# Chunk 0 of a windowed-attention kernel: first loads in 4 KB rows, attention ahead of the weight conversions, and half of the weight subtractions moved from GpSimd to VectorE

## The chip, the cores and the metric

The kernel runs on one core of one Trainium2 chip. The metric is the device time of one execution in microseconds (us). In the text PE is TensorE, DVE is VectorE, ACT is ScalarE, POOL is GpSimd, and SP is SyncE, which issues the DMAs.

## What is computed

The reference is attention followed by a feed-forward block, all in float32. For each of 4 batches and 8 heads, 768 queries of 64 elements attend to the keys less than 16 positions away and to 24 summaries of the keys (the elementwise maximum over blocks of 32; the values' summary is the mean):

```python
k_sum = k.reshape(B, H, nb, block, D).max(axis=3)
v_sum = v.reshape(B, H, nb, block, D).mean(axis=3)
scores_l = scale * np.matmul(q, k.transpose(0, 1, 3, 2))          # kept where |i - j| < 16
scores_s = scale * np.einsum('bhsd,bhnd->bhsn', q, k_sum) + np.log(block)
a = softmax(np.concatenate([scores_l_masked, scores_s], axis=-1))
x = np.matmul(a, np.concatenate([v, v_sum], axis=2))              # 3072 tokens x 512
r = np.maximum(x @ w_in, 0.0)                                     # w_in 512 x 2048
out = (s * (r * r) + b) @ w_out                                   # w_out 2048 x 512
```

## The kernel before

**Tiling.** The 3072 tokens are 12 chunks `c` of 256 tokens, three for each batch. The 8 heads are 4 pairs `p`; a pair of heads of one chunk is a unit. The 2048 hidden features are 16 blocks `f` of 128.

**Attention of a unit** goes through the engines in these steps; the letters are those of the string `FIRST_ORDER`, and a digit behind a letter is the unit's `p`. K (`k_max`, L158): DVE takes the maxima of the keys. S (`scores`, L241): PE. M (`masked`, L264): DVE adds the mask and takes the maximum. E (`exps`, L281): ACT. N (`normalize`, L289): DVE divides by the sums. F (`fill_v`, L233): the 24 mean values are copied into the tile of values. T (`transposes`, L297): PE. C (`turned`, L303): ACT copies the transposed probabilities from PSUM. V (`values`, L307): PE. X (`attended`, L320): ACT copies the result, a block of x; from chunk 1 on it is split into a high part `xh` and a rest `xl`, which DVE subtracts. For chunk 0 the means of the values come from twelve matmuls over plain rows of v (R, `mean_of_rows`, L196) with one ACT copy behind them.

**Feed-forward.** For a chunk and an `f`, `hidden` (L335) multiplies x by a block of w_in, `activate` (L349) makes g = s r^2 + b, and `project` (L367) adds g times a block of w_out into two PSUM banks; `evict` (L384) stores them after f = 15. Chunk 0 uses whole float32 weights `w_f` and float32 x. From chunk 1 on there are three matmuls of a faster kind in place of one: with the rounded weight `wh` and its rest `wl`, and x and g split alike.

**Weights** arrive as 64-bit numbers, one block of w_in ("in") and one of w_out ("out") for each f, 512 KB each. `scale_weights` (L113; A in the string) is two ACT operations, `convert_weights` (L121; D for both halves of an f) is three DVE operations for each half (L132, L134, L136). `split_weights` (L138) later makes `wh` on ACT (L145) and `wl` by a subtraction (L147): on DVE for "in", on POOL for "out".

**Order.** The program is a plan of numbered steps; step i holds `hidden(c, f)` for i = 16 c + f, the `activate` of the same, and `project` of the one two steps back. The engines run their own instructions in the plan's order. Within a step the kinds follow each other as L393 says: loads, weight work (scaling, conversion, splitting), attention, hidden, PE's attention, activate, project, evict. Conversion of f stands at step f - 2, scaling at f - 3, splitting at 13 + f. The attention of chunk 1 is spread over steps 0 to 15, that of chunk c > 1 begins at step 16 (c - 1) - 2. Ahead of step 0 all loads of chunk 0 and the first twelve weights are issued on SP (L401 to L408), then the work in the string `FIRST_ORDER` (L397) is run.

**Buffers.** The pool `slots` has 16 buffers of 4 KB a partition: first the rows of v and the raw weights, later the pairs of rounded weights. `wring` holds the converted weights and the rests; the rest of an "out" block goes into the buffer of the "in" block of the same f.

Of the kernel before, what the change touches and what calls it, by code (L numbers as in the profile page):

```python
# [44 lines left out]
def windowed_attention_then_relu2_ffn(ctx, tc, qk, vwin, kt, vt, vrow, wp, s, b, out):  # L45
# [92 lines left out]
    def split_weights(key):  # L138
# [8 lines left out]
        (nc.vector if key[0] == "in" else nc.gpsimd).tensor_tensor(  # L147
# [10 lines left out]
    def k_max(bi, p):  # L158
        ksum[bi, p] = p2.tile([P, NB], F32, name="ksum", bufs=8)
        raw = kraw[bi, p]  # L160
        nc.vector.tensor_reduce(
            ksum[bi, p], raw.rearrange("p (n t) -> p n t", t=BLOCK), axis=AX.X, op=ALU.max
        )
# [25 lines left out]
    def load_rows():  # L189

        for j in range(3):
            t = slots.tile([P, 2, DM], F32, name="vn", tag="slot")
            nc.sync.dma_start(t, vrow[:, 2 * j : 2 * j + 2, :])
            vn.append(t)

    def mean_of_rows():  # L196
        pm = ps_po.tile([P, DM], F32, name="pm", tag="po")
        for j in range(6):
            nc.tensor.matmul(
                pm[:KR], mean4[:, 20 - 4 * j : 20 - 4 * j + KR], vn[j // 2][:, j % 2],  # L200
                start=(j == 0), stop=(j == 5),
            )
# [1 line left out]
        nc.scalar.copy(vsum[0][WIN:KR].rearrange("p h d -> p (h d)"), pm[WIN:KR])
# [327 lines left out]
```

## Time and profile before

| | |
|---|---|
| three runs | 668.0 us median (667.82 to 669.35) |
| the profiled execution's own time | 667.75 us |
| its span, first to last instruction | 666.1 us |
| busy: PE, DVE, ACT, POOL | 637.8, 327.3, 331.7, 173.2 us |
| read from memory, written | 55.90 MB, 6.29 MB |
| 16 subtractions `wl_out` on POOL (L147) | 23.2 us, 1451 ns each |

The profile is of one execution. A row of a timeline gives the start, the duration, engine, line, operation, the tile written and those read, the shape, and in brackets how long the engine was idle before it and for what it waited. A row of the chain of waits gives the start, the time that this piece adds to the chain, and the piece. A group of instructions has its busy time and the mean of one, then the idle time before its instructions and who ended it. In a timeline two instructions of one engine can overlap by a pipeline's length, so that an engine's pace is read from starts, or from the chain.

### The profile page before, as it was taken

Reading aid. Unit: us, or ns where it says so; the run is one execution under the profiler, and the core shown is the slowest. Engines: PE = TensorE matmul, PEld = TensorE weight load, DVE = VectorE, ACT = ScalarE, POOL = GpSimd, SP = SyncE. Lnnn points to the kernel's source line nnn. Section 1 sums busy time; section 2 is a strip of 40 time slices with the busy share of each in tenths; the row PEclk is TensorE's granted clock in tenths of the full one; section 3 lists DMA queues with packets and bytes.
Section 4 is the critical chain, followed back from the end, with each engine's and each line's share of the span. In section 5 each row is a group of like instructions: output and inputs, shape, how many; then the busy total and the mean of one; then the engine's idle time right before and its main releaser. Section 6 shows DMA issues by size and latency. Waiting matters only on the chain.

```text
span 666.1 us, 13961 instructions
## 1 busy us (share of the span) xinstructions
PE 637.8 (96%) x5164; PEld 555.1 (83%) x5164; DVE 327.3 (49%) x1086; ACT 331.7 (50%) x972; POOL 173.2 (26%) x342
## 2 busy tenths in 40 slices
PE   4698989989999999999999999999999999999997
PEld 2465657878999999999989999999999999999996
DVE  2799995467443343346543343345643343443221
ACT  2598967564444444444444444444543543543322
POOL 3000034553322312313313313313313313312221
PEclk9798999989999999999999999999999999999999
DMA  7999602304510320503520320503520320100000
GB/s 235 357 378 372 190 1 80 102 1 124 172 59 2 106 66 1 180 1 104 181 70 2 102 70 1 180 1 100 185 71 1 101 71 1 57 2 2 31 1 32
DMA packets 26100, 63.25 MB, mean 95 GB/s; under 512 B 3952, under 2 KB 4464, under 8 KB 26032
## 3 DMA queue, kind: packets, MB, share of 16 engines
q1 hardware_dynamic: 25968, 62.35, 28.6%
q8 instruction: 41, 0.67, 0.4%
q14 instruction: 27, 0.22, 0.1%
q0 software_dynamic: 64, 0.00, 0.0%
HBM read 55.90 MB, written 6.29 MB: 93 GB/s over the span
## 4 chain that ended last, share of the span: by engine, by line
PE 82%; DVE 9%; ACT 3%; DMA 2%; POOL 1%; issue 1%; SPq 1%; POOLq 0%; ACTq 0%
PE po L379 37%; PE ph L345 36%; PE pav L315 4%; PE pt L301 3%; PE ps L258 3%; DMA kraw<-in_kt_dram 2%; DVE wf_out L136 1%; DVE wf_out L134 1%; DVE wf_in L134 1%; DVE wf_in L136 1%; DVE pr L295 1%; DVE pr L272 1%; ACT pr L285 1%; POOL wl_out L147 1%; DVE wl_in L147 1%
## 5 line engine op out<-in xcount | busy, mean ns | idle before, releaser
L352 ACT ACTIVATE r<-ph 128x256 f32<-128x256 f32 x192 | 73.3, 382 | 293.2 <-PE ph L345 255.8
L362 DVE CAST gh<-g 128x256 fp32r<-128x256 f32 x176 | 52.2, 297 | 302.5 <-POOL g L360 283.9
L360 POOL TENSOR_SCALAR g<-r,s_col,b_col 128x256 f32<-128x256 f32 x176 | 99.7, 567 | 374.4 <-ACT r L353 318.0
L379 PE MATMUL po<-wh,gl 128*128 128x512 f32 x352 | 143.6, 408 | 0.0
L379 PE MATMUL po<-wh,gh 128*128 128x512 f32 x352 | 139.1, 395 | 0.0
L379 PE MATMUL po<-wl_out,gh 128*128 128x512 f32 x352 | 138.4, 393 | 0.0
L345 PEld LDWEIGHTS ph<-xh,wl_in 128*128 128x128 f32 x704 | 108.1, 189 | 16.2 <-ACT r L353 0.7
L345 PE MATMUL ph<-xh,wl_in 128*128 128x256 f32 x704 | 113.5, 284 | 0.0
L345 PE MATMUL ph<-xl,wh 128*128 128x256 f32 x704 | 109.3, 277 | 0.0
L345 PE MATMUL ph<-xh,wh 128*128 128x256 f32 x704 | 108.8, 277 | 0.0
L345 PEld LDWEIGHTS ph<-xl,wh 128*128 128x128 f32 x704 | 95.3, 189 | 0.0
L345 PEld LDWEIGHTS ph<-xh,wh 128*128 128x128 f32 x704 | 92.9, 188 | 0.0
L353 ACT ACTIVATE r<-r 128x256 f32<-128x256 f32 x192 | 80.2, 418 | 6.1
L285 ACT ACTIVATE pr<-pr,mn 128x120 f32<-128x120 f32 x192 | 73.2, 383 | 14.0 <-DVE mn L272 14.0
L364 DVE TENSOR_TENSOR gl<-g,gh 128x256 fp32r<-128x256 f32 x176 | 76.5, 435 | 6.0
L379 PEld LDWEIGHTS po<-wh,gh 128*128 128x128 f32 x352 | 66.4, 189 | 14.0
L379 PEld LDWEIGHTS po<-wh,gl 128*128 128x128 f32 x352 | 66.4, 189 | 10.8 <-DVE gh L362 2.7
L379 PEld LDWEIGHTS po<-wl_out,gh 128*128 128x128 f32 x352 | 66.6, 189 | 7.9
L147 POOL TENSOR_TENSOR wl_out<-wf_out,wh 128x512 fp32r<-128x512 f32 x16 | 23.2, 1451 | 108.9 <-ACT wh L145 83.8
L301 PE MATMUL pt<-ident,pr 128*120 128x128 f32 x192 | 30.5, 283 | 9.2 <-DVE pr L295 9.1
L295 DVE TENSOR_TENSOR pr<-pr,rs 128x480 f32<-128x480 f32 x48 | 35.5, 741 | 1.7
L285 ACT ACTIVATION_READ_ACCUMULATOR pr<-pr,mn 128x1 f32 x192 | 36.0, 188 | 0.0
(67 smaller groups left out, 621.9 us busy)
## 6 DMA issues: line engine op xcount, KB each, us to landing
wraw<-in_wp_dram SPq DMA_DIRECT2D x32, 512.0 KB, 10.2
qk<-in_qk_dram SPq DMA_DIRECT2D x44, 368.0 KB, 4.8
vw<-in_vwin_dram SPq DMA_DIRECT2D x48, 192.0 KB, 4.1
kraw<-in_kt_dram SPq DMA_DIRECT2D x16, 384.0 KB, 3.4
out_dram<-o SPq DMA_DIRECT2D x24, 256.0 KB, 2.0
vraw<-in_vt_dram SPq DMA_DIRECT2D x12, 252.0 KB, 4.4
vraw<-in_vt_dram SPq DMA_DIRECT2D x6, 264.0 KB, 6.7
vn<-in_vrow_dram SPq DMA_DIRECT2D x3, 512.0 KB, 10.6
```

What stands on the lines that cost most here:

```text
L147: (nc.vector if key[0] == "in" else nc.gpsimd).tensor_tensor(w_l[key], whole, w_h[key].bitcast(F32), ALU.subtract)
L285: nc.scalar.activation(pr, pr, AF.Exp, bias=mn_of[c, p][:, n : n + 1], scale=-1.0, accum_out=sm_of[c, p][:, n : n + 1])
L295: nc.vector.tensor_tensor(pr, pr, rs.unsqueeze(2).to_broadcast([P, 4, KR]), ALU.mult)
L301: nc.tensor.transpose(pt_of[c, p][:KR, n * P : (n + 1) * P], pr[:, n, :], ident)
L315: nc.tensor.matmul(o[64 * e : 64 * e + 64, i * SUB : (i + 1) * SUB], vw[:, e, i, :], pT[:, e * T + i * SUB : e * T + (i + 1) * SUB], start ...
L345: nc.tensor.matmul(ph, w[:, kc * P : (kc + 1) * P], x[:, kc], start=(n == 0), stop=(n == len(terms) - 1))
L352: nc.scalar.activation(r, ph, AF.Relu)
L353: nc.scalar.activation(r, r, AF.Square)
L360: nc.gpsimd.tensor_scalar(g, r, s_col, b_col, ALU.mult, ALU.add)
L362: nc.vector.tensor_copy(gh, g)
L364: nc.vector.tensor_tensor(gl, g, gh.bitcast(F32), ALU.subtract)
L379: nc.tensor.matmul(po[t], a[:, t * P : (t + 1) * P], w, start=(f == 0 and n == 0), stop=(f == NF - 1 and n == len(terms) - 1),)
```

## The change

It has these parts:

- **First loads.** For chunk 0 the keys of a pair (3 KB a partition) and its queries (1 KB) were two loads into two pools. They become one load of 4 KB rows (`load_first`) into the pool `slots`. The rows of v are laid out in memory so that each of the three loads is contiguous. The order of the loads is written into `FIRST_ORDER` in small letters (q: keys and queries, r: rows of v, v: windows of values, s: s and b, i and o: weights, u: the first unit of chunk 1), between the other work. s and b come in one load on SP in place of two on POOL.
- **Order of chunk 0.** Scores of the next unit now stand ahead of the mask of the one before. The mean matmuls are three groups of four (R0 to R2), with the copy apart (R3). F, V and X of all units come at the end. The first conversions are one half at a time (B0, B1: the in and the out half of f = 0; behind A and B the digit counts halves, 2f and 2f + 1), and the first fill of chunk 1's keys (G0) moves ahead. Eight blocks are scaled ahead of step 0 in place of six.
- **Buffers of chunk 0.** Probabilities go to the pool `stage`, two of the transposed tiles to `slots`, and the results of odd units to the PSUM banks of `project`.
- **Order in a step.** Splitting gets a kind of its own ahead of attention; attention stands ahead of scaling and conversion.
- **Subtraction.** `wl` of the "out" blocks is made on DVE, like that of the "in" blocks.
- The identity matrix is made later on POOL, `ksum` has 12 buffers in place of 8, and `pr` is 16 columns wider.

The diff without its unchanged lines (the laying out of inputs at its end is cut to the two lines that matter):

```diff
-    make_identity(nc, ident)
-    s_col = const.tile([P, 1], F32, name="s_col")
-    b_col = const.tile([P, 1], F32, name="b_col")
-    nc.gpsimd.dma_start(s_col, s.partition_broadcast(P))
-    nc.gpsimd.dma_start(b_col, b.partition_broadcast(P))
+    sb_col = const.tile([P, 2], F32, name="sb_col")
+    s_col, b_col = sb_col[:, 0:1], sb_col[:, 1:2]
...
+    make_identity(nc, ident)
...
-        (nc.vector if key[0] == "in" else nc.gpsimd).tensor_tensor(
+        nc.vector.tensor_tensor(
...
-    def load_rows():
-        for j in range(3):
-            t = slots.tile([P, 2, DM], F32, name="vn", tag="slot")
-            nc.sync.dma_start(t, vrow[:, 2 * j : 2 * j + 2, :])
-            vn.append(t)
-    def mean_of_rows():
-        pm = ps_po.tile([P, DM], F32, name="pm", tag="po")
-        for j in range(6):
+    def load_rows(j):
+        t = slots.tile([P, 2, DM], F32, name="vn", tag="slot")
+        nc.sync.dma_start(t, vrow[j])
+        vn.append(t)
+    def load_scalars():
+        nc.sync.dma_start(sb_col, sb.partition_broadcast(P))
+    pm = []
+    def mean_of_rows(n):
+        if n == 0:
+            pm.append(ps_po.tile([P, DM], F32, name="pm", tag="po"))
+        for j in (2 * n, 2 * n + 1):
...
-                pm[:KR], mean4[:, 20 - 4 * j : 20 - 4 * j + KR], vn[j // 2][:, j % 2],
+                pm[0][:KR], mean4[:, 20 - 4 * j : 20 - 4 * j + KR], vn[n][:, j % 2],
...
+    def mean_done():
...
-        nc.scalar.copy(vsum[0][WIN:KR].rearrange("p h d -> p (h d)"), pm[WIN:KR])
+        nc.scalar.copy(vsum[0][WIN:KR].rearrange("p h d -> p (h d)"), pm[0][WIN:KR])
...
+    def load_first(p):
+        t = slots.tile([P, S + T], F32, name="kq", tag="slot")
+        nc.sync.dma_start(t, kq[p])
+        kraw[0, p], qk_t[0, p] = t[:, :S], (t[:, S:], None)
...
-        if c == 0:
-            nc.sync.dma_start(t[:, 0:T], qk[c, p, :, 0:T])
-        else:
-            nc.sync.dma_start(t, qk[c, p])
+        nc.sync.dma_start(t, qk[c - 1, p])
...
-        if j == 0:
-            pr_of[c, p] = p2.tile([P, 4, KR], F32, name="pr")
+        if j == 0 and c == 0:
+            t = stage.tile([P, 4 * KR + 8], F32, name="pr0", tag="stage")
+            pr_of[c, p] = t[:, : 4 * KR].rearrange("p (n k) -> p n k", k=KR)
+            mn_of[c, p], sm_of[c, p] = t[:, 4 * KR : 4 * KR + 4], t[:, 4 * KR + 4 :]
+        elif j == 0:
+            t = p2.tile([P, 4 * KR + 16], F32, name="pr")
+            pr_of[c, p] = t[:, : 4 * KR].rearrange("p (n k) -> p n k", k=KR)
...
-        pT_of[c, p] = p2.tile([KR, 4 * P], F32, name="pT")
+        if c == 0 and p > 1:
+            pT_of[c, p] = slots.tile([KR, 4 * P], F32, name="pT0", tag="slot")
+        else:
+            pT_of[c, p] = p2.tile([KR, 4 * P], F32, name="pT")
...
-        if c < 2 or p % 2 == 0:
+        if c == 0 and p % 2:
+            o_of[c, p] = ps_po.tile([P, DM], F32, name="pav", tag="po")
+        elif c < 2 or p % 2 == 0:
...
-            o_of[c, p + 1] = o_of[c, p][:, T:]
+            if c > 1:
+                o_of[c, p + 1] = o_of[c, p][:, T:]
...
-    LOAD, WEIGHTS, ATT, HID, PE_ATT, CHAIN, PROJ, EVICT = range(8)
-    FIRST, FIRST_SCALED, FIRST_TURNED = -100, 6, 2
+    LOAD, SPLIT, ATT, WEIGHTS, HID, PE_ATT, CHAIN, PROJ, EVICT = range(9)
+    FIRST, FIRST_SCALED, FIRST_TURNED = -100, 8, 2
...
-        "K0 S0 M0 E0 K1 S1 M1 E1 R0 K2 N0 F0 T0 C0 S2 M2 E2 N1 F1 V0 X0 T1 C1 K3 S3 M3 E3 V1 X1 "
-        "A0 N2 F2 T2 C2 A1 V2 X2 N3 F3 T3 C3 D0 A2 V3 X3 A3 D1 A4 A5"
+        "q0 q1 q2 r0 q3 r1 r2 i0 v0 v1 o0 v2 v3 s0 i1 o1 "
+        "K0 S0 K1 S1 M0 E0 K2 i2 M1 E1 o2 R0 S2 N0 T0 C0 K3 M2 E2 S3 i3 u0 N1 T1 R1 C1 M3 E3 R2 N2 T2 A0 C2 o3 i4 o4 "
+        "N3 T3 R3 C3 F0 V0 F1 X0 V1 F2 B0 A1 X1 V2 F3 X2 V3 B1 X3 A2 A3 G0 D1 i5 o5 A4 A5 A6 A7"
...
-    for n, (fn, args) in enumerate(
-        [(load_k, (0, 0)), (load_unit, (0, 0)), (load_k, (0, 1)), (load_unit, (0, 1)), (load_rows, ())]
-        + [(load_values, (0, 0)), (load_k, (0, 2)), (load_unit, (0, 2)), (load_values, (0, 1))]
-        + [(load_k, (0, 3)), (load_unit, (0, 3)), (load_values, (0, 2)), (load_values, (0, 3))]
-        + [(load_weights, ((side, f),)) for f in range(2) for side in ("in", "out")] + [(load_unit, (1, 0))]
-        + [(load_weights, ((side, f),)) for f in range(2, 6) for side in ("in", "out")]
-    ):
-        at(FIRST, n, fn, *args)
+    loads = {
+        "q": load_first, "r": load_rows, "v": lambda p: load_values(0, p), "s": lambda _: load_scalars(),
+        "i": lambda f: load_weights(("in", f)), "o": lambda f: load_weights(("out", f)),
+        "u": lambda p: load_unit(1, p),
+    }
...
-        if kind == "R":
-            at(FIRST + 1, n, mean_of_rows)
+        if kind in loads:
+            at(FIRST + 1, n, loads[kind], i)
+        elif kind == "R":
+            at(FIRST + 1, n, *((mean_of_rows, i) if i < 3 else (mean_done,)))
...
+        elif kind == "G":
+            at(FIRST + 1, n, fill_k, 1, i)
+        elif kind == "B":
+            at(FIRST + 1, n, convert_weights, ("in" if i % 2 == 0 else "out", i // 2))
...
-            if (c, p) != (1, 0):
+            if (c, p) not in ((1, 0),):
...
-            at(base - (1 if c > 1 else 2), ATT, fill_k, c, p)
+            if (c, p) != (1, 0):
+                at(base - (1 if c > 1 else 2), ATT, fill_k, c, p)
...
-            at(NF - 3 + f, WEIGHTS, split_weights, (side, f))
+            at(NF - 3 + f, SPLIT, split_weights, (side, f))
...
+    kq = np.concatenate([kT[0], qT[0, :, :, :T]], axis=-1)
-    vrow = v[0].transpose(1, 0, 2).reshape(6, P, H * D).transpose(1, 0, 2)
+    vrow = v[0].transpose(1, 0, 2).reshape(3, 2, P, H * D).transpose(0, 2, 1, 3)
```

More of the change, by code (lines that the diff above doesn't have):

```diff
@@ L44, in windowed_attention_then_relu2_ffn @@
 @with_exitstack
-def windowed_attention_then_relu2_ffn(ctx, tc, qk, vwin, kt, vt, vrow, wp, s, b, out):
+def windowed_attention_then_relu2_ffn(ctx, tc, qk, vwin, kt, vt, kq, vrow, wp, sb, out):
     nc = tc.nc
@@ L158, in k_max @@
     def k_max(bi, p):
-        ksum[bi, p] = p2.tile([P, NB], F32, name="ksum", bufs=8)
+        ksum[bi, p] = p2.tile([P, NB], F32, name="ksum", bufs=12)
         raw = kraw[bi, p]
@@ L480, in windowed_attention_then_relu2_ffn, with laid_out @@
                 fn(*args)
-def laid_out(q, k, v, moe_w_in, moe_w_out, **_):
+def laid_out(q, k, v, moe_w_in, moe_w_out, moe_s, moe_b):
     import numpy as np
@@ L490, in laid_out @@
     qT, kT = turn(q), turn(k)
-    qk = np.zeros((NC, NPAIR, P, T + NSUB * KR), np.float32)
+    kq = np.concatenate([kT[0], qT[0, :, :, :T]], axis=-1)
+    qk = np.zeros((NC - 1, NPAIR, P, T + NSUB * KR), np.float32)
     vwin = np.zeros((NC, NPAIR, WIN, 2, NSUB, D), np.float32)
@@ L494, in laid_out @@
         bi, ci = divmod(c, PER_B)
-        qk[c, :, :, :T] = qT[bi, :, :, ci * T : (ci + 1) * T]
-        kw = qk[c, :, :, T:].reshape(NPAIR, P, NSUB, KR)
+        kw = np.zeros((NPAIR, P, NSUB, KR), np.float32)
         for i in range(NSUB):
@@ L500, in laid_out @@
             vwin[c, :, :, :, i] = v[bi, :, w : w + WIN].reshape(NPAIR, 2, WIN, D).transpose(0, 2, 1, 3)
-        qk[c, :, :, T:] = kw.reshape(NPAIR, P, NSUB * KR)
+        if c > 0:
+            qk[c - 1] = np.concatenate(
+                [qT[bi, :, :, ci * T : (ci + 1) * T], kw.reshape(NPAIR, P, NSUB * KR)], axis=-1
+            )
     vt = v.reshape(B, 2, 4, NB, BLOCK, D).transpose(0, 1, 2, 3, 5, 4).reshape(B, 2, 4 * NB, D, BLOCK)
-    vrow = v[0].transpose(1, 0, 2).reshape(6, P, H * D).transpose(1, 0, 2)
+    vrow = v[0].transpose(1, 0, 2).reshape(3, 2, P, H * D).transpose(0, 2, 1, 3)
     w_in = moe_w_in.view(np.int64).reshape(NKC, P, NF, P).transpose(2, 1, 0, 3).reshape(NF, P, 512)
     w_out = moe_w_out.view(np.int64).reshape(NF, P, DM)
-    return {"qk": qk, "vwin": vwin, "kt": kT, "vt": vt, "vrow": vrow, "wp": np.stack([w_in, w_out], axis=1)}
+    return {"qk": qk, "vwin": vwin, "kt": kT, "vt": vt, "kq": kq, "vrow": vrow, "wp": np.stack([w_in, w_out], axis=1),
+            "sb": np.concatenate([moe_s, moe_b])}
 _OUTS = [((3072, 512), "float32")]
@@ L519 @@
     sent = laid_out(**{n: _np.ascontiguousarray(a) for n, a in inputs.items()})
-    sent |= {"s": inputs["moe_s"], "b": inputs["moe_b"]}
     for name, a in sent.items():
```

## Prediction

> **What bounds the kernel now.** I read the page first, its busy shares and slices, then the matmul timeline for landmarks, then the chain that ended last and the groups of each engine stage by stage.
>
> ```profile
> span 666.1 us, 13961 instructions
> ...
> PE 637.8 (96%) x5164; PEld 555.1 (83%) x5164; DVE 327.3 (49%) x1086; ACT 331.7 (50%) x972; POOL 173.2 (26%) x342
> ...
> PE   4698989989999999999999999999999999999997
> ```
>
> PE is busy 96% of the span, and from the tenth slice (of 16.65 us) to the last but one every slice is full. What can still be won lies ahead of that, in slices 1 to 9, some 150 us: all digits below 9 stand there.
>
> ```profile
> 101.47 1.89 PE L345 MATMUL ph<-x,wf_in 128*128 128x256 f32 x8
> ...
> 157.31 0.50 PE L379 MATMUL po<-wh,gl 128*128 128x512 f32 x1
> ```
>
> These are my two landmarks. The row at 101.47 is hidden(0,15), the last f of chunk 0. The row at 157.31, project(1,12), lies where the full slices begin. Behind it nothing is changed and PE has no gap to lose, so the end moves as this row moves. I sum in two stages: to 101.47, and from there to 157.31.
>
> **Stage one, the first chunk's loads.** Slices of 0.6 us from the DMA view of 0 to 24 us, and the rows that start the work:
>
> ```profile
> DMA  0009693855214999999999999998998898899999
> GB/s 0 0 0 189 246 359 127 154 77 176 99 74 151 366 376 411 408 420 398 304 277 285 306 307 273 273 302 227 270 213 225 270 331 259 249 314 335 355 382 321
> ...
> 10.64 0.95 DVE L161 TENSOR_REDUCE ksum<-kraw 128x24 f32<-128x768 f32 x1 [2.80 <-DMA kraw<-in_kt_dram]
> 12.89 6.76 PE L199 MATMUL pm<-vn,mean 128*120 128x512 f32 x12
> 18.36 0.95 DVE L161 TENSOR_REDUCE ksum<-kraw 128x24 f32<-128x768 f32 x1 [4.52 <-DMA kraw<-in_kt_dram]
> ...
> 19.69 0.58 ACT L204 COPY vsum<-pm 24x512 f32<-24x512 f32 x1 [4.80 <-PE pm L199]
> ...
> 25.98 1.12 PE L315 MATMUL pav<-pT,vw 120*64 120x64 f32 x16
> 26.04 0.28 DVE L272 CUSTOM_DVE_ANT_0 pr<-ps,mask_first 128x120 f32<-128x120 f32 x1 [0.84 <-PE ps L262]
> ...
> 26.86 0.17 DVE L292 TENSOR_SCALAR rs<-sums 128x4 f32<-128x4 f32 x1
> ...
> 27.96 0.49 DVE L236 COPY vw<-vsum 24x256 f32<-24x256 f32 x2
> ...
> 34.01 0.37 ACT L328 COPY x<-pav 128x256 f32<-128x256 f32 x1
> ```
>
> K2 (the reduce at 18.36) waits for its load and stands ahead of N0 on DVE, so the whole attention of chunk 0 hangs on that landing; it ends with X3, at 34.01 + 0.37 = 34.38. The DMA engines are not idle meanwhile: from 11 to 19 us their digit is 8 or 9 at some 280 GB/s. Between 7.8 and 10.8 us, when the 4 KB rows of vn are under way, the same engines move about 400.
>
> After the change the first seven loads (q0 to q3, r0 to r2) are 3.67 MB in 4 KB rows. Up to 7.8 us the row adds to 1.0 MB (13 slices times 0.6 us), and I keep that slow beginning. The other 2.7 MB take 6.5 us at 410 GB/s or 9.6 at 280, so r2 lands between 14.3 and 17.4. The second unit's load I leave at the row it has now, 10.6, because nothing shows that it would come sooner. I take the faster rate: its row is of 4 KB rows, as all these loads will be.
>
> The Trainium skill speaks against this: by its page "DMA: Bandwidth & Descriptors", section Specifications, rows of 512 B and more already run at line rate, so longer ones would win nothing. The two rates in the GB/s row disagree with it, though other things than row length also differ there. What it would do to the sum is the first rival below.
>
> From 10.6 DVE has in its queue K1 M0 K2 M1 N0 K3 M2 N1 M3 N2 N3. K is 0.95 by its row; M 0.82 (26.04 to 26.86), N 1.10 (26.86 to 27.96). That is 3 x 0.95 + 4 x 0.82 + 4 x 1.10 = 10.5 us, to 21.1 if nothing waits. (M0 was done before that landing; behind K1 it costs its 0.8 here.) PE is the other side: the twelve mean matmuls took 6.76 us, and are now in three groups between scores and transposes. The pav row at 25.98 shows 1.12 us for work that takes 0.6 to 0.7 later, so a PE that idles runs at half speed here. From S1 at 11.6 PE has those 6.8 us and five scores and transposes ahead of the end of the means: 22 with 0.7 for each of the five, 23.9 with 1.1, 26 with 2 us of waits for DVE between them. I take 24, by the pav row. A0, ahead of C2 on ACT, waits for the eighth load, 1.3 to 1.9 behind r2 and so at 19.3 at the latest, when ACT still has exponentials to do: nothing. Then the vsum copy 0.6, F0 0.5, four V of 1.1 with B0 (1.5) on DVE in between, and X3 0.4: X3 ends near **30**, range 28 to 33, against 34.38. Nothing is counted for the rest. The s and b loads leave POOL for SP, behind the eleven loads that attention needs, and are used at the first g. The identity is made later on POOL, its first user is T0, past 14 us. The new places of pr, pT and pav free buffers sooner and take none that is due. On SP the load of f=7 now waits for the conversion of f=0, which frees its slot, and holds all later loads behind it; but it is used seven conversions later, 21 us, and a weight load lands in 10.2 (page, part 6):
>
> ```profile
> wraw<-in_wp_dram SPq DMA_DIRECT2D x32, 512.0 KB, 10.2
> ```
>
> Without that cover each step would wait, and this is what I would look for first.
>
> **Stage one, the conversions.** From DVE's timeline and the chain, the pieces of a conversion; then groups of DVE between 37.8 and 97.6; then the timeline again:
>
> ```profile
> 37.84 0.42 DVE L132 TENSOR_SCALAR wf_in<-wraw 128x512 uint32<-128x512 uint32 x1
> ...
> 38.91 0.57 ACT wraw L118
> ...
> 41.33 0.34 DVE wf_in L132
> ...
> 42.00 0.60 DVE wf_in L134
> ...
> 43.20 0.60 DVE wf_in L136
> ...
> L136 DVE CUSTOM_DVE_ANT_0 wf_out<-wraw,wf_out 128x1024 uint16<-128x1024 uint16 x15 | 10.2, 683 | 0.0
> L295 DVE TENSOR_TENSOR pr<-pr,rs 128x480 f32<-128x480 f32 x4 | 2.6, 659 | 0.1
> ...
> 91.96 1.53 DVE L236 COPY vw<-vsum 24x256 f32<-24x256 f32 x2
> ...
> 97.53 0.42 DVE L330 TENSOR_TENSOR xl<-pav,xh 128x256 fp32r<-128x256 f32 x1
> 98.06 0.69 PE L315 MATMUL pav<-pT,vw 120*64 120x64 f32 x16 [1.85 <-ACT wh L145]
> ```
>
> The pieces of an out half take as long as those of its in half: one f is 2 x 1.54 = 3.1 us. The groups stand there with no idle time ahead of them, so from f=2 to 97.53, when f=15 is done, DVE does not rest. This stage is DVE's, whatever order its queue has. In the first conversion after X3, D1, ACT must scale both halves (A2, A3) behind X3: 3 x 0.57 to the first piece of the second half, then 0.34 + 4 x 0.60. f=2 can start 4.45 after X3. Today it starts at 37.84 (the first row here), 3.46 after X3. So it comes to 30 + 4.45 = 34.45, a gain of 3.4.
>
> The DVE work from there is 97.53 - 37.84 = 59.7. It loses 1.0 (the two copies at 91.96 take 1.53 beside POOL's first subtraction, and took 0.49 at 27.96) and gains 0.6 (the first lower output weight, now ahead of conversion 15). It ends at 34.45 + 59.3 = 93.75. Putting attention first changes no sum on DVE, but it takes away what follows: V of the last unit at 98.06 waited 1.85 although its named releaser is ACT's; the xl at 97.53, which frees pav, was queued behind conversion 15. So today hidden(0,15) starts 3.9 after its weights. With xl ahead of the conversion PE reaches it in time: its own work from 30 is 15 hidden x 1.74 + 13 project x 1.72 (the first rows of the next fence), 4 V of 0.69, 4 T of 0.72, 3 x 1.05 for the scores of six units (rows here and below) and 3 for half speed, twice what the wait in stage two costs: to 90, so it is not late. Hidden(0,15) then starts 0.75 after its weights, at **94.5** instead of 101.47: **-7.0**.
>
> **Stage two, lower output weights.** From the chain, PE's and POOL's timelines and DVE's groups between 101.4 and 157.3:
>
> ```profile
> 92.77 1.72 PE po L379 x4
> 94.48 1.74 PE ph L345 x8
> ...
> 127.22 1.05 PE L258 MATMUL ps<-qk 64*64 64x120 f32 x32 [1.14 <-POOL qk L231]
> ...
> 136.24 1.30 POOL L147 TENSOR_TENSOR wl_out<-wf_out,wh 128x512 fp32r<-128x512 f32 x1 [1.56 <-DVE wl_in L147]
> 137.52 0.56 POOL L360 TENSOR_SCALAR g<-r,s_col,b_col 128x256 f32<-128x256 f32 x1
> ...
> 141.57 0.72 PE L301 MATMUL pt<-ident,pr 128*120 128x128 f32 x4 [2.05 <-DVE pr L295]
> 142.29 2.56 PE po L379 x6
> 144.86 1.71 PE ph L345 x12
> ...
> 161.72 1.39 PE ph L345 x12
> ...
> 169.07 1.39 PE po L379 x6
> ...
> 138.87 0.60 DVE wl_in L147
> ...
> L295 DVE TENSOR_TENSOR pr<-pr,rs 128x480 f32<-128x480 f32 x4 | 6.6, 1648 | 0.1
> L362 DVE CAST gh<-g 128x256 fp32r<-128x256 f32 x14 | 4.1, 295 | 19.7 <-POOL g L360 19.7
> ```
>
> On POOL a subtraction waits 1.56 and takes 1.3 in front of g, and DVE waits 19.7 us in all for g. The normalization takes 1.65 here and 0.66 before. On DVE each of the 16 subtractions costs 0.60, as wl_in's does in the chain. POOL keeps g and the fills. What goes for PE: the wait of 1.14 for the fill queued behind POOL's subtraction, the 2.05 for the normalization, and the slow matmuls behind that wait, 2.56 + 1.71 against 1.39 + 1.39 for the same counts in the later rows, 1.5. Together 4.7. The next things to be late are the split's own steps on DVE, put ahead of attention: 13 x 0.6 = 7.8 more on an engine that idles 19.7 us here for g alone, so I give back 0.5: **-4.2**.
>
> Here a rule speaks against the change: the Trainium skill's page "SBUF — State Buffer", section Who interferes with whom, has a DVE operation with two SBUF inputs and a GpSimd operation that reads SBUF exclude each other for a whole instruction. The 1648 ns beside 659 ns agree with it. By it a subtraction on DVE can hold up g on POOL. In this queue gh of a step, which waits for g, stands ahead of the next step's subtractions, so g and they hardly meet; if they always did, it is the last rival.
>
> **The sum.** 667.75 (profiled execution, 666.1 of span and 1.65 around it) - 7.0 - 4.2 = 656.55. The median of the runs is 0.25 above the profiled one, so I predict **656.8**.
>
> **Rivals.** First, longer rows do not speed the loads and X3 stays at 34.4: f=2 starts at 38.85, hidden(0,15) at 98.9, a gain of 2.6; with 4.2 of stage two 661.2. For it: nothing shows q1 sooner. Against: the two rates. By the Trainium skill's rule on row length (DMA: Bandwidth & Descriptors) this would be the outcome.
>
> Second, nearly all that PE loses comes back: X3 at 28 brings 2 more, stage two without the 0.5 and with the smaller losses of the switch to the split weights (about 1) 1.5 more: 653.3 or a little below. For it: PE has some 4 us in hand ahead of hidden(0,15). Against: twelve mean matmuls at half speed.
>
> Third, no change: the eight large loads in flight share the engines evenly, so that q1 and q2 land near 13 instead of 10.6, X3 falls at 36 and the loss eats what stage one brings (hidden(0,15) at 100.5, -1.0), while the freed POOL waits are replaced by DVE's: 666 to 668. For it: the second load now waits till 10.6 although it was issued second in its kind.
>
> Fourth, slower: DVE becomes the bound in steps 13 to 28. All 16 subtractions lie on the path (9.6), and on 13 steps g waits for one as well (7.8): 668.0 - 7.0 + 17.4 = 678.4. It decides when DVE's step is longer than PE's, 2.78 plus attention. Today DVE idles at least 19.7 of 55.8 us there, against 7.8 added, so I give it little.
>
> **How the numbers follow.** Forecast (653.5 to 660) 0.47; little from the loads (660 to 665) 0.23; nearly all back (under 653.5) 0.17; no change 0.06; slower 0.07. A difference of 0.3%, 2 us, is about what a measurement of this kernel can tell from none. Faster is the first three, 0.87. The range 650 to 663 leaves out the last two cases, part of the second and the far end of the third, together near 0.2.
>
> **What would show it.** Right: GB/s near 400 from 8 us on; X3 at 28 to 33; no idle DVE between D1 and conversion 15, which ends at 92 to 97; hidden(0,15) within 1.5 us behind it; no POOL subtraction, L295 back near 0.7 us between 95 and 150, no PE wait above 0.5 us there; the 157.31 row at 146. Wrong: K1 later than 12 us, PE waiting for wf pieces by more than a step, or gh waiting for POOL as long as today.

## The result and the profile after

The changed kernel takes **651.93 us** (median, 650.97 to 652.7), the kernel before 667.91 beside it: a ratio of 0.9762, interval 0.9733 to 0.979. It is faster by 16 us. The prediction said 656.8, range 650 to 663. The profiled execution took 652.11 us with a span of 650.4, against 667.75 and 666.1, so the traces account for 15.7.

Where those went is read from the same landmarks as in the prediction. First the rows of PE, hidden(0,15) and project(1,12):

```profile
91.19 1.89 PE L364 MATMUL ph<-x,wf_in 128*128 128x256 f32 x8
...
141.77 0.50 PE L398 MATMUL po<-wh,gl 128*128 128x512 f32 x1
```

Stage one ends at 91.19 in place of 101.47, 10.28 sooner (predicted 7.0). Stage two lasts 50.58 in place of 55.84, 5.26 less (predicted 4.2). Behind it nothing moved: 10.28 + 5.26 = 15.54 of 15.7.

Stage one in its pieces. The DMA view of 0 to 24 us (slices of 0.6 us), then ACT's timeline with the end of X3, then DVE's with K1, with the first row of f=2 and with the first row behind conversion 15:

```profile
DMA  0008989999999999999999999999999999999999
GB/s 0 0 0 191 348 294 369 416 382 410 382 430 403 423 430 423 417 403 423 416 416 314 256 297 259 324 331 277 281 294 311 382 396 417 410 410 403 417 410 399
```

```profile
26.06 0.37 ACT L347 COPY x<-pav 128x256 f32<-128x256 f32 x1 [1.22 <-PE pav L334]
```

```profile
5.59 0.95 DVE L159 TENSOR_REDUCE ksum<-kq 128x24 f32<-128x768 f32 x1 [0.32 <-DMA kq<-in_kq_dram]
...
30.91 0.42 DVE L130 TENSOR_SCALAR wf_in<-wraw 128x512 uint32<-128x512 uint32 x1
...
90.67 0.41 DVE L375 TENSOR_SCALAR g<-r,sb_col 128x256 f32<-128x256 f32 x1
```

The stretch of 74 to 176 GB/s that the loads of the kernel before went through from 3.6 to 7.8 us is gone, and the second unit's keys are there at 5.59 and not at 10.64. X3 ends at 26.43 (before 34.38), f=2 starts at 30.91 (37.84), DVE then works without a gap for 59.76 us (59.7), and hidden(0,15) follows 0.52 us later (3.94). From 12.6 to 18.6 us the loads still move only some 290 GB/s, with all engines busy.

Stage two, the groups of DVE between 91 and 142 us (busy time, mean ns, idle time ahead and what ended it):

```profile
L145 DVE TENSOR_TENSOR wl_out<-wf_out,wh 128x512 fp32r<-128x512 f32 x15 | 10.4, 694 | 1.6
...
L381 DVE CAST gh<-g 128x256 fp32r<-128x256 f32 x15 | 4.8, 319 | 5.2 <-POOL g L379 5.1
...
L308 DVE TENSOR_TENSOR pr<-pr,rs 128x480 f32<-128x480 f32 x4 | 2.7, 687 | 0.1
```

The normalization is back at 687 ns from 1648, DVE waits 5.1 us for g in place of 19.7, and PE has no wait left in this stage.

### The profile page after: what moved, and what is told of

It reads as the page before. It is cut to its first block, busy times and chain, and to the rows that moved or that the text cites. A ratio compares the mean times of both kernels' runs of the same rounds, so it can differ in the third digit from the quotient of the medians.

```text
span 650.4 us, 13951 instructions
## 1 busy us (share of the span) xinstructions
PE 633.2 (97%) x5164; PEld 551.1 (85%) x5164; DVE 333.8 (51%) x1102; ACT 331.1 (51%) x972; POOL 152.5 (23%) x324
## 4 chain that ended last, share of the span: by engine, by line
PE 88%; DVE 9%; DMA 1%; issue 1%; ACT 1%; SPq 0%; DVEq 0%
PE po L398 39%; PE ph L364 38%; PE pav L334 4%; PE ps L266 3%; PE pt L314 3%; DVE wf_in L132 1%; DVE wf_out L134 1%; DVE wf_out L132 1%; PE pm L202 1%; DMA vn<-in_vrow_dram 1%; DVE wf_in L134 1%; DVE wf_in L130 1%; DVE wf_out L130 1%; DVE g L375 1%; DVE vw L244 1%
## 5 line engine op out<-in xcount | busy, mean ns | idle before, releaser
L379 POOL TENSOR_SCALAR g<-r,sb_col 128x256 f32<-128x256 f32 x176 | 100.4, 570 | 423.8 <-ACT r L372 354.4
L298 ACT ACTIVATE pr<-pr,mn 128x120 f32<-128x120 f32 x176 | 67.1, 383 | 3.4 <-DVE mn L285 3.4
L364 PEld LDWEIGHTS ph<-x,wf_in 128*128 128x128 f32 x128 | 24.8, 199 | 15.9 <-issue 6.3
L244 POOL COPY vw<-vsum 24x256 f32<-24x256 f32 x80 | 36.6, 497 | 1.3
L364 PE MATMUL ph<-x,wf_in 128*128 128x256 f32 x128 | 32.4, 400 | 4.5 <-DVE wf_in L134 3.7
L298 ACT ACTIVATION_READ_ACCUMULATOR pr<-pr,mn 128x1 f32 x176 | 33.1, 188 | 0.0
```

What stands on the lines that cost most here:

```text
L244: filler(c).tensor_copy(vw_t[c, p][WIN:KR, e], vsum[bi][WIN : WIN + NB, 2 * p + e, :].unsqueeze(1).to_broadcast([NB, NSUB, D]),)
L298: nc.scalar.activation(pr, pr, AF.Exp, bias=mn_of[c, p][:, n : n + 1], scale=-1.0, accum_out=sm_of[c, p][:, n : n + 1])
L364: nc.tensor.matmul(ph, w[:, kc * P : (kc + 1) * P], x[:, kc], start=(n == 0), stop=(n == len(terms) - 1))
L379: nc.gpsimd.tensor_scalar(g, r, s_col, b_col, ALU.mult, ALU.add)
```

## The experiments

Each kernel was traced and timed beside the kernel before, and its ratio is to that. "X3" is the end of X3, "f=2" the first row of that conversion, "h15" and "p12" are hidden(0,15) and project(1,12), from the profiled execution of each.

By the intervals of the ratios only e3, e5, e6 and e7 are clear of the kernel after; for the others the readings rest on rows of one traced execution each. How far such a row carries can be seen where the work up to X3 is the same: X3 ends at 26.43, 26.57 and 26.15 in the kernel after, e3 and e4, and at 34.38 and 34.49 in the kernel before and e6.

| kernel | time, us | ratio, interval | span | X3 | f=2 | h15 | p12 |
|---|---|---|---|---|---|---|---|
| before | 667.91 | 1 | 666.1 | 34.38 | 37.84 | 101.47 | 157.31 |
| after | 651.93 | 0.9762 (0.9733-0.9790) | 650.4 | 26.43 | 30.91 | 91.19 | 141.77 |
| e1 | 654.64 | 0.9791 (0.9776-0.9805) | 652.8 | 28.14 | 32.99 | 93.47 | 144.05 |
| e2 | 653.07 | 0.9768 (0.9752-0.9784) | 651.6 | 27.68 | 32.18 | 92.39 | 143.01 |
| e3 | 657.89 | 0.9844 (0.9827-0.9861) | 656.2 | 26.57 | 31.06 | 91.78 | 147.62 |
| e4 | 654.91 | 0.9797 (0.9778-0.9816) | 653.2 | 26.15 | 30.64 | 93.97 | 144.54 |
| e5 | 656.52 | 0.9834 (0.9805-0.9863) | 652.5 | 28.48 | 32.98 | 93.25 | 143.81 |
| e6 | 661.48 | 0.9913 (0.9887-0.9939) | 660.7 | 34.49 | 37.96 | 101.26 | 151.90 |
| e7 | 666.38 | 0.9991 (0.9978-1.0005) | 664.9 | 31.58 | 35.05 | 100.50 | 156.44 |
| e8 | 651.80 | 0.9771 (0.9743-0.9798) | 649.8 | 25.61 | 30.23 | 90.52 | 141.23 |
| e9 | 652.11 | 0.9759 (0.9741-0.9778) | 651.1 | 28.64 | 29.29 | 91.90 | 142.47 |
| e10 | 652.28 | 0.9763 (0.9744-0.9782) | 650.7 | 26.80 | 31.29 | 91.53 | 142.08 |
| e11 | 652.68 | 0.9772 (0.9756-0.9787) | 650.9 | 25.70 | 31.24 | 91.81 | 142.36 |
| e12 | 650.52 | 0.9746 (0.9732-0.9761) | 648.4 | 24.11 | 27.45 | 89.22 | 139.80 |

### The loads: e1, e2, e5, e7

**e1**, the kernel after with the scalars on POOL again:

```diff
+    nc.gpsimd.dma_start(s_col, sb[0:1].partition_broadcast(P))
+    nc.gpsimd.dma_start(b_col, sb[1:2].partition_broadcast(P))
...
-        "q0 q1 q2 r0 q3 r1 r2 i0 v0 v1 o0 v2 v3 s0 i1 o1 "
+        "q0 q1 q2 r0 q3 r1 r2 i0 v0 v1 o0 v2 v3 i1 o1 "
```

> The changed kernel, but s and b are again two loads issued on POOL at the start, as in the kernel before; all loads of keys, queries and rows as after the change. Theory (the slow stretch of the DMA engines from 4 to 8 us comes with the two POOL loads): the rate falls below 200 GB/s from 4 to 8 us again, K1 starts near 10 instead of 5.6, X3 ends 2 to 4 us later, and so does the kernel, 654 to 656. Rival (the slow stretch comes with the short rows and small loads): K1 stays within 1 us of 5.6 and the time within 1 us of the changed kernel.

The two rows of its DMA view (the upper one is the busy share of the 16 engines, in tenths):

```profile
DMA  0009979930882169999999999999999999999999
GB/s 0 0 0 150 348 300 389 403 157 28 322 287 96 41 267 423 416 416 430 423 410 416 437 396 413 253 219 263 246 276 365 236 249 270 256 345 393 396 403 416
```

Two holes are back, at 4.8 to 6.0 us (157, 28) and 7.2 to 8.4 (96, 41), one for each of two loads that carry 512 bytes. What is missing in the four slices against 410 is some 1.9 us of transfer, and X3 is later by 1.71. In the holes the engines' busy share falls to 0 to 3 tenths: they mostly stand still, with large loads in flight. Why they stand is in no run. K1 did not go to 10: in DVE's timeline q1 still lands at 5.65, and it is q2 that the holes hold up (the kernel after has K2 at 7.56, with no wait).

```profile
5.65 0.95 DVE L161 TENSOR_REDUCE ksum<-kq 128x24 f32<-128x768 f32 x1 [0.29 <-DMA kq<-in_kq_dram]
...
9.82 0.95 DVE L161 TENSOR_REDUCE ksum<-kq 128x24 f32<-128x768 f32 x1 [2.00 <-DMA kq<-in_kq_dram]
```

**e2**, the kernel after with the 3 KB and the 1 KB rows loaded apart:

```diff
-        nc.sync.dma_start(t, kq[p])
+        nc.sync.dma_start(t[:, :S], kt[0, p])
+        nc.sync.dma_start(t[:, S:], kq[p][:, S:])
```

> The changed kernel, but each load of 4 KB rows of keys and queries is made in two, 3 KB rows and 1 KB rows, in the same place and order; s and b stay on SP. Theory (POOL's loads were the cause): K1 at 5.6 to 7, the time within 1.5 us of the changed kernel. Rival (row length): K1 at 9 to 10.6, the rate from 4 to 8 us below 200 GB/s, the time 2 to 4 us longer, 654 to 656.

K1, from DVE's timeline, and the GB/s row of its DMA view:

```profile
6.47 0.95 DVE L159 TENSOR_REDUCE ksum<-kq 128x24 f32<-128x768 f32 x1 [1.61 <-DMA kq<-in_kt_dram]
...
GB/s 0 0 0 215 357 277 210 316 280 302 278 222 237 396 403 406 406 422 428 423 403 437 393 369 232 270 239 218 352 287 226 240 256 273 314 410 403 423 403 403
```

K1 came at 6.47 and X3 1.25 later, p12 1.24 later, as the theory had it. But it is not nothing: from 3.6 to 7.8 us the loads move 264 GB/s on average, where the kernel after moves 399. The edit makes the rows shorter and the loads more in number, and no run parts the two.

**e5**, the two edits of e1 and e2 together:

> The kernel after, with the two scalars loaded by POOL at the start as in the kernel before, and each kq load made as two: 3 KB rows of keys and 1 KB rows of scores. That gives back both of the change's edits to the loads of chunk 0, and leaves all else. Theory (the short rows and POOL's tiny loads are together what held the second load of keys till 10.6 in the kernel before; each alone cost 1.2 to 1.7 us at X3): the first chunk's maximum of pair 1 comes at 9 to 11 instead of 5.59, X3 ends at 29 to 31 instead of 26.43, the time is 656 to 658 on this chip where the kernel after would have 652 to 653. Rival (the two costs are the same stall and do not add): X3 at 28 to 28.5, 654 to 655. Second rival (the eight large loads take turns in another way because vn and the weights now follow in other places, and this alone brought pair 1 early): X3 below 28.

K1, from DVE's timeline:

```profile
8.23 0.95 DVE L161 TENSOR_REDUCE ksum<-kq 128x24 f32<-128x768 f32 x1 [3.29 <-DMA kq<-in_kt_dram]
```

It came at 8.23 and X3 at 28.48. By the trace the two costs do not add up in full: X3 is 2.05 later than in the kernel after, p12 2.04. The traced execution (654.24) is the fastest of four, the others took 655.9 to 657.6; what made those slower is in no trace, and stays open. Of the 7.95 us that X3 gained, these two edits explain 2.05. The other 5.9 belong to the rest of the change to chunk 0, its order and that of its loads, which no run took apart further. Nor do the two edits bring K1 back to 10.64: it comes at 5.65 with e1's alone, at 6.47 with e2's alone and at 8.23 with both.

**e7**, the kernel *before* with its two scalar loads on SP behind the values:

```diff
-    nc.gpsimd.dma_start(s_col, s.partition_broadcast(P))
-    nc.gpsimd.dma_start(b_col, b.partition_broadcast(P))
+    def load_scalars():
+        nc.sync.dma_start(s_col, s.partition_broadcast(P))
+        nc.sync.dma_start(b_col, b.partition_broadcast(P))
...
-        + [(load_k, (0, 3)), (load_unit, (0, 3)), (load_values, (0, 2)), (load_values, (0, 3))]
+        + [(load_k, (0, 3)), (load_unit, (0, 3)), (load_values, (0, 2)), (load_values, (0, 3)), (load_scalars, ())]
```

> The kernel before with one edit: the two scalars are loaded by SP behind the values of chunk 0, not by POOL at the start. Theory (POOL's tiny loads at the start cause the stall of the large loads between 4 and 8 us): the gap in the bytes between 4 and 8 us is gone, the maximum of pair 1 comes at 6 to 8.5 instead of 10.6, and X3 ends 1.5 to 3 us sooner than 34.4, the time 665 to 667.5. Rival (the stall belongs to the beginning of any execution of this kernel, or to the 1 KB rows): gap and 10.6 as before, the time within 0.15% of the kernel before.

The GB/s row of its DMA view:

```profile
GB/s 0 0 0 189 230 376 294 364 271 266 311 350 343 365 362 406 367 265 251 316 290 295 232 307 271 270 156 113 91 134 212 396 389 341 348 198 266 410 416 417
```

The stall at 4 to 8 us is gone, K1 comes at 7.25, X3 2.8 sooner. The hole has moved with the loads, to 15.6 to 18.6 us, and SP issues them here: it is the tiny load, not the queue. Yet the time is the same. f=2 starts 2.79 sooner, h15 only 0.97. Here are PE's windows around the wait for the last V (length, PE busy, granted clock, DMA share, GB/s), first of e7, then of the kernel before:

```profile
93.40:95.40 2.00, 0.02 (x1) 1.00 0.00 0
95.40:97.50 2.10, 2.06 (x48) 0.75 0.00 0
97.50:100.50 3.00, 3.00 (x9) 0.60 0.02 5
```

```profile
96.20:98.00 1.80, 0.01 (x1) 1.00 0.00 0
98.00:99.60 1.60, 1.54 (x48) 1.00 0.00 0
99.60:101.40 1.80, 1.80 (x11) 1.00 0.03 9
```

In e7 V waited 2.02 us and the clock fell to 0.75 and 0.60: from V to hidden(0,15) PE needed 5.06. In the kernel before V waited 1.85, the clock stayed at 1.00, and the same work took 3.41. So 1.65 of the 2.62 us by which V starts sooner were lost behind a wait that the order of attention and conversions makes.

### The order in a step and the subtraction: e3, e4, e6

**e4**, the kernel after with weights ahead of attention again:

```diff
-    LOAD, SPLIT, ATT, WEIGHTS, HID, PE_ATT, CHAIN, PROJ, EVICT = range(9)
+    LOAD, SPLIT, WEIGHTS, ATT, HID, PE_ATT, CHAIN, PROJ, EVICT = range(9)
```

> The changed kernel, but within a step scaling and conversion stand ahead of attention again; splitting still stands first. Theory: DVE's sum does not change, conversion 15 ends within 1 us of 90.7, but PE waits for transposes and for the last V (its bank is freed behind conversion 15), hidden(0,15) starts 2 to 5 us later than 91.2 and the total is 654 to 657. Rival (DVE bounds this stage whatever the order, and PE catches up): within 1 us of the changed kernel.

From PE's timeline:

```profile
90.55 0.69 PE L334 MATMUL pav<-pT,vw 120*64 120x64 f32 x16 [1.43 <-ACT wh L143]
...
93.97 1.89 PE L364 MATMUL ph<-x,wf_in 128*128 128x256 f32 x8
```

The last piece of conversion 15 starts even a little sooner than in the kernel after (89.41 against 90.07), but V waits 1.43 and hidden(0,15) starts 2.78 later. p12 moves by 2.77: the whole price is the lag at the end of stage one.

**e3**, the kernel after with `wl_out` on POOL:

```diff
-        nc.vector.tensor_tensor(
+        (nc.vector if key[0] == "in" else nc.gpsimd).tensor_tensor(
```

> The changed kernel, but the lower output weights are subtracted on POOL again. Theory of stage two: PE waits come back at the fill of chunk 2's keys (1 us), at a normalization (2 us, with slow matmuls behind it), project(1,12) starts 4 to 6 us later than 141.77, total 656 to 658. Rival (stage two gained because PE and DVE arrive in better order, not because of POOL): less than 1.5 us longer.

Groups between 91 and 148 us, then the waits of PE in its timeline:

```profile
L145 POOL TENSOR_TENSOR wl_out<-wf_out,wh 128x512 fp32r<-128x512 f32 x15 | 19.3, 1285 | 29.2 <-DVE wl_in L145 16.8 <-DVE rs L305 4.7 <-ACT wh L143 3.1
...
L308 DVE TENSOR_TENSOR pr<-pr,rs 128x480 f32<-128x480 f32 x4 | 6.6, 1646 | 0.1
...
L381 DVE CAST gh<-g 128x256 fp32r<-128x256 f32 x14 | 4.1, 295 | 19.0 <-POOL g L379 19.0
```

```profile
117.54 1.05 PE L266 MATMUL ps<-qk 64*64 64x120 f32 x32 [1.04 <-POOL qk L239]
131.89 0.62 PE L314 MATMUL pt<-ident,pr 128*120 128x128 f32 x4 [2.05 <-DVE pr L308]
```

Stage two lasts 147.62 - 91.78 = 55.84, to the hundredth what it lasted before, and the two waits that the prediction named are back with 1.04 and 2.05.

**e6**, the kernel before with that one edit:

```diff
-        (nc.vector if key[0] == "in" else nc.gpsimd).tensor_tensor(
+        nc.vector.tensor_tensor(
```

> The kernel before with one edit: the lower output weights subtracted on DVE instead of POOL. Theory (stage two's gain is this edit's alone): hidden(0,15) stays within 0.5 of 101.5, the row of project(1,12) comes 50 to 51.5 us after it instead of 55.8, so 663 to 664.5 against 668 to 669. Rival (the subtractions need attention placed ahead of conversions, otherwise DVE's queue holds up attention): stage two 52 to 55, over 665.

```profile
101.26 1.89 PE L345 MATMUL ph<-x,wf_in 128*128 128x256 f32 x8
...
151.90 0.50 PE L379 MATMUL po<-wh,gl 128*128 128x512 f32 x1
```

Stage one is as before (101.26; both rows are of PE's timeline), stage two lasts 151.90 - 101.26 = 50.64. The edit is worth 5.2 of the 5.26 and needs no other part of the change. The time, 661.48, lay below the 663 to 664.5 expected, as the kernel before did beside it (666.6).

### What is left: e8 to e12

**e8** reorders chunk 0 of the kernel after (the part that differs):

```diff
-        "K0 S0 K1 S1 M0 E0 K2 i2 M1 E1 o2 R0 S2 N0 T0 C0 K3 M2 E2 S3 i3 u0 N1 T1 R1 C1 M3 E3 R2 N2 T2 A0 C2 o3 i4 o4 "
-        "N3 T3 R3 C3 F0 V0 F1 X0 V1 F2 B0 A1 X1 V2 F3 X2 V3 B1 X3 A2 A3 G0 D1 i5 o5 A4 A5 A6 A7"
+        "K0 S0 K1 S1 M0 E0 K2 i2 M1 E1 o2 R0 S2 N0 T0 A0 C0 K3 M2 E2 S3 i3 u0 R1 N1 T1 C1 M3 E3 R2 N2 T2 R3 C2 B0 N3 T3 "
+        "A1 C3 o3 i4 o4 F0 V0 F1 X0 V1 F2 X1 V2 F3 X2 B1 V3 A2 X3 A3 G0 D1 i5 o5 A4 A5 A6 A7"
```

> The kernel after with the order of chunk 0 written otherwise: the first scaling of weights ahead of the first copy on ACT, the second mean matmuls ahead of the second transposes on PE, the copy of the means ahead of the third turned copy, and the first conversions between the normalizations on DVE. Theory (DVE's work decides from the first conversion on, and what it can do of it while it waits in chunk 0 comes off the time at one to one): DVE's idle time of some 5.5 us before 22 us is filled by up to 3, the row of f=2 comes at 28 to 29.5 instead of 30.9, hidden(0,15) at 88 to 90 instead of 91.2, stage two unchanged at 50.6, so 649 to 651 where the kernel after has 652 to 653. Rival (PE is late at hidden(0,15), since stage one is now bound by it): conversion 15 ends sooner and hidden(0,15) does not follow, less than 1 us in all.

```profile
27.03 0.21 DVE L239 COPY qk<-ksum 128x96 f32<-128x96 f32 x1 [1.99 <-DMA qk<-in_qk_dram]
```

B0 moved from 22.88 to 18.40, but f=2 gained 0.7 alone: G0 (the row of DVE's timeline) now waits 1.99 for the load of unit (1,0), and D1 is queued behind it. The loads had become late next. The time moved by less than 1 us, as the rival said, but not for the rival's reason, a late PE.

**e9** went further: S2 and S3 ahead of R0, the mean matmuls between the transposes, A0 to A2 and B0 to B2 early, u0 ahead of two weight halves, G0 behind B3. In place of the same two lines of the kernel after:

```diff
+        "K0 S0 K1 S1 M0 E0 K2 S2 M1 E1 i2 N0 T0 C0 K3 M2 E2 u0 S3 R0 N1 T1 M3 E3 o2 N2 N3 A0 C1 R1 T2 B0 A1 C2 R2 T3 B1 "
+        "i3 A2 R3 C3 o3 i4 o4 B2 F0 V0 F1 X0 V1 F2 X1 V2 A3 F3 X2 V3 B3 X3 G0 i5 o5 A4 A5 A6 A7"
```

> The kernel after with chunk 0 ordered anew, from what the last order left idle: the scores of units 2 and 3 ahead of the first mean matmuls on PE, the mean matmuls spread between the transposes, the scalings right behind the last exponentials on ACT, the first three conversions ahead of the fills on DVE, the load of unit (1,0) ahead of two of the weight halves, and its fill behind the second conversion. Theory (DVE's work decides: f=2 starts once X3 and the conversions of f=0 and f=1 are done): DVE's idle time before f=2 falls from 10.4 us in the kernel of the last order (4.4 of them the first load) to about 6, f=2 starts at 26.5 to 28 instead of 30.2, and hidden(0,15) at 87 to 88.5 instead of 90.5, so 648 to 650 where the kernel after would have 652. Rival (PE is the bound by then: it idles 4.6 us in all between 30 and 90 in the kernel of the last order): conversion 15 ends sooner, hidden(0,15) stays above 89.5, and the time within 1 us of the kernel after.

From its timelines of ACT, DVE and PE:

```profile
19.16 0.67 ACT L116 ACTIVATE wraw<-wraw 128x512 f32<-128x512 f32 x1 [1.64 <-DMA wraw<-in_wp_dram]
```

```profile
19.86 0.43 DVE L130 TENSOR_SCALAR wf_out<-wraw 128x512 uint32<-128x512 uint32 x1 [1.27 <-ACT wraw L116]
```

```profile
24.90 3.32 PE L334 MATMUL pav<-pT,vw 120*64 120x64 f32 x64 [3.33 <-DVE vw L244]
```

It was no gain. The early scalings stood on ACT ahead of the copy of the means and waited for weights still in flight; the fills came late, V waited 3.33, and X3 ended 2.2 later than in the kernel after. (f=2 starts sooner, at 29.29, but its second half then waits 0.69 for ACT, and h15 is 0.71 later.) Both the theory's numbers (87 to 88.5) and its reason failed: ahead of f=2 DVE alone is not the bound.

**e10** and **e11** ask about the loads once more. e10 pads the windows of values from 96 to 128 partitions; e11 does without the scalars' load (they ride in the rows of the units' loads, and POOL copies them out). First the diff of e10, then the core of e11's:

```diff
-        nc.sync.dma_start(v[0:WIN], vwin[c, p])
+        nc.sync.dma_start(v, vwin[c, p])
...
-    vwin = np.zeros((NC, NPAIR, WIN, 2, NSUB, D), np.float32)
+    vwin = np.zeros((NC, NPAIR, P, 2, NSUB, D), np.float32)
```

```diff
-        t = p3.tile([P, T + NSUB * KR], F32, name="qk", bufs=4)
+        t = p3.tile([P, T + NSUB * KR + 2], F32, name="qk", bufs=4)
...
+        if (c, p) == (1, 0):
+            nc.gpsimd.tensor_copy(sb_col, t[:, T + NSUB * KR :])
...
+    qk[..., T + NSUB * KR :] = np.concatenate([moe_s, moe_b])
```

> The kernel after with the value windows padded by zeros from 96 to 128 partitions, in DRAM and in the loads (256 KB instead of 192 for each of them), and nothing else. Theory (the stretch from 12.6 to 18.6 us at about 290 GB/s is the value windows': their 96 partitions leave part of the 16 engines out, or their shorter rows slow all that is in flight): with 128 partitions the stretch is at 380 to 420 GB/s, if the partitions are what matters; at 290 as before, if the 2 KB rows do. Rival (the stretch belongs to the tiny load of the scalars, issued at 11.26): 290 as before. The time within 1 us of the kernel after either way, since DVE is not fed by the loads in that stretch alone.

> The kernel after without the load of the two scalars: they stand as two more columns in each row of the units' loads, and POOL copies them once from the load of unit (1,0) to their place. Theory (the value windows make the stretch at 290 GB/s): the stretch from 12.6 to 18.6 us stays, X3 within 0.4 of 26.4, the time within 1 us of the kernel after. Rival (128 rows of 8 bytes slow the large loads for some us wherever they stand, as two loads of 128 rows of 4 bytes did at the start and, in the kernel before with its scalars on SP, at 16 to 18 us): the stretch is gone or shorter by half, and the loads of the weights land 1 to 2 us sooner.

The GB/s rows of the DMA views, first of e10, then of e11:

```profile
GB/s 0 0 0 198 328 328 417 410 321 355 396 375 396 403 410 416 423 416 416 417 416 393 417 413 416 396 382 311 89 86 355 396 396 416 423 416 430 410 417 417
```

```profile
GB/s 0 0 0 177 341 430 416 362 307 382 389 416 396 403 423 423 410 396 430 437 396 338 249 290 229 218 311 256 270 294 246 273 379 335 362 423 410 410 389 423
```

With 128 partitions, and rows still of 2 KB, the slow stretch is gone (393 to 417 from 12.6 to 15.6 us); without the scalars' load it stays (218 to 338). The 96 partitions make it. In e10 the scalars' load now stands out as a hole of its own, 89 and 86 at 16.8 to 18.0 us. Neither moved the time. By 24 us e10 had moved 8.29 MB, 0.26 of it padding, and the kernel after 8.14: the higher rate brought no more of what is used. In e11 X3 was 0.7 sooner, and G0 then waited 1.46 for unit (1,0).

**e12** takes both, and an order that starts from e9's waits: S2 alone ahead of R0, A0 behind E2, A1 behind C1, A2 behind C2, and "B2 G0 B3" for "G0 D1".

```diff
+        "K0 S0 K1 S1 M0 E0 K2 i2 M1 E1 o2 S2 R0 N0 T0 K3 M2 E2 A0 C0 N1 N2 S3 u0 i3 M3 E3 R1 T1 C1 A1 B0 R2 R3 T2 C2 N3 "
+        "T3 A2 C3 o3 i4 o4 F0 V0 F1 X0 V1 F2 X1 V2 F3 X2 B1 V3 X3 A3 B2 G0 B3 i5 o5 A4 A5 A6 A7"
```

> The kernel after with what the other runs left idle taken together: the value windows padded to 128 partitions, no load of the scalars, and a third order of chunk 0, which keeps the mean matmuls early on PE as the kernel after has them, moves only the scores of unit 2 ahead of them, and places a scaling on ACT where its half has landed by the rows of the last runs. Theory (loads, ACT and DVE take turns as the bound ahead of f=2; in the second order ACT waited 1.64 and 0.98 us for weights to land, and the fills came late behind it): no load is waited for behind the first, X3 ends at 24 to 25, f=2 starts at 27 to 28.5 instead of 30.9, hidden(0,15) at 88 to 89.5 instead of 91.2, and the time is 648.5 to 650.5 where the kernel after has 652. Rival (PE takes over as the bound between 30 and 90: it idles about 4.6 us there, and cannot give back more than it has): f=2 starts that early and hidden(0,15) stays above 90, the time within 1 us of the kernel after.

Rows of DVE (f=2, and the next fill) and of PE:

```profile
27.45 0.42 DVE L130 TENSOR_SCALAR wf_in<-wraw 128x512 uint32<-128x512 uint32 x1
...
33.21 0.21 DVE L238 COPY qk<-ksum 128x96 f32<-128x96 f32 x1 [1.41 <-DMA qk<-in_qk_dram]
```

```profile
36.04 3.02 PE L363 MATMUL ph<-x,wf_in 128*128 128x256 f32 x8 [2.21 <-DVE wf_in L134]
...
89.22 1.89 PE L363 MATMUL ph<-x,wf_in 128*128 128x256 f32 x8
```

f=2 starts 3.46 sooner than in the kernel after and h15 1.97: DVE waits 1.41 for the next unit's load, and PE's wait of 2.21 is followed by a hidden of 3.02 where 1.9 is usual. The landmarks lay where the theory put them, the time 0.02 above its range, and a load is still waited for. 650.52 is the lowest median of all, 1.4 below the kernel after; the intervals of the two ratios overlap, so it is not shown to be faster.

## Why the prediction was nearly right, and where it was off

The time lay in the range, 4.9 below the predicted value and below the forecast's own interval of 653.5 to 660. The sum said -11.2 where the traces have -15.5: 3.3 are missing in stage one and 1.1 in stage two. Of the cases named, the second rival (nearly all comes back, 653.3 or a little below, chance 0.17) is the one that came. Of the signs, GB/s near 400 held only to 12.6 us; X3 (28 to 33), the end of conversion 15 (92 to 97) and project(1,12) (146) all came sooner, at 26.43, 90.7 and 141.77. The parts of stage one add up to its error: 3.57 from X3 and 0.23 from hidden(0,15), less 0.03 for the step behind X3 and 0.46 for DVE's work, 3.3 in all.

- **First loads, the mis-sized term.** The step that failed is "The second unit's load I leave at the row it has now, 10.6", with "I keep that slow beginning" and "Nothing is counted for the rest" ahead of and behind it. Measured: 5.59, and X3 at 26.43 against the 30 predicted. The steps behind K1 were a little too short in the sum, not too long. The last mean matmuls are this row of PE:

```profile
16.24 3.60 PE L202 MATMUL pm<-vn,mean 128*120 128x512 f32 x8
```

From the end of K1 (5.59 + 0.95) to their end at 19.84 it took 13.3 us where the sum has 12.4, and from there to X3 6.6 where it has 6.0. So the 3.57 by which X3 came sooner than predicted are the 5.05 of K1 (10.64 to 5.59) less some 1.5. Two edits to the loads, counted at nothing or as a rate only, are part of those 5.05: the two loads of 512 bytes that the change took off the start (e1, and e7 from the other side), and the rows of 4 KB (e2). Together they are worth 2.6 at K1 and 2.05 at X3 (e5). The other 2.4 at K1 lie in the rest of the change to the loads, and their cause stays open. The diff showed the two small loads go; that they are used late was taken as a reason to count nothing, but the cost fell on the large loads beside them.

- **Row length.** The rates of 280 and 400 GB/s were read as rows of 1 to 3 KB against 4 KB. For the stretch of the kernel after that is not the cause: it comes from loads to 96 partitions (e10). In the kernel before, such loads and shorter rows were in flight together, and no run parts them there. Loads in shorter rows do run slower at the start (264 against 399 GB/s in e2), and cost 1.25 us at X3. The first rival's rule, in the Trainium skill's "DMA: Bandwidth & Descriptors", section Specifications, that rows of 512 B and more already run at line rate, fits e10's 2 KB rows and does not by itself give e2's start; the rival's outcome did not come, because X3's gain hung on other things. The Trainium skill's page "SBUF — State Buffer", section Door 1: The DMA port swizzle, has partitions 0 to 63 share 8 of 16 ports, 27.2 GB/s each, and 64 to 127 the other 8. By it 96 partitions put two thirds of their bytes on half the ports, an estimate of 27.2 x 8 x 3/2 = 326 GB/s; the 256 to 331 of that stretch agree with the direction and lie mostly below it, with other loads mixed in.
- **From X3 to f=2:** 4.45 predicted, 4.48 measured. **DVE's work from there:** 59.3 against 59.76, with no idle time. **hidden(0,15) behind its weights:** 0.75 against 0.52; e4 shows that this is the order's doing, 2.78 us.
- **Stage two:** 4.2 against 5.26. The 4.7 of named waits were right (e3 gives them back), the 0.5 taken off again for DVE's extra work was not lost, and 0.6 more came from smaller losses, which no run took apart. e6 shows that the subtraction alone does it. The fourth rival (DVE becomes the bound) had nothing: no PE wait is left, and gh waits less for g than it did.
- **Third rival** (the large loads take turns and land late): K1 shows the opposite.

Undone one at a time, the parts cost p12 5.85 (e3), 2.77 (e4) and 2.04 (e5). With 15.54 in all, 4.9 is left for the order of chunk 0 and its loads, if the parts add, which e5 and e7 show that they need not.

## What to carry to other kernels

Price every DMA that an edit moves by what the loads beside it lose, and not by its bytes or by who waits for it: here 512 bytes spread over 128 partitions cost them about 1 us, in which some 400 KB would have moved. A gain at the head of a chain is worth only what the next queue hands on: e7 won 2.8 us at the loads and lost most of it behind one wait that the order made, so parts that gain little alone, like these loads, are worth trying together with the order. And when two rates differ, list all that was in flight in both stretches before one cause is chosen.
